# Linear attention feeding a gated layer: unread matrix products after each group of products in the first batch's attention

## The chip, the cores and the metric

The kernel runs on one core of one Trainium2 chip. The metric is the device time of one execution in microseconds (us). Before the change it is 1277.1 us, the median of 3 runs (1275.62 to 1277.16).

The core's engines named here are TensorE (PE in the profile; PEld is its weight load), VectorE (DVE), ScalarE (ACT), GpSimd (POOL) and SyncE (SP), which here only issues DMA transfers. Each engine works through its own instruction list in order. TensorE's clock is granted at one of two levels, 1.2 GHz (0.50 in the profile) or 2.4 GHz (1.00).

## The reference

Attention is linear: queries and keys go through random features, so that a head needs one 128x64 matrix `kv` and no table of scores. Its output, 4608 tokens by 512, is the input of a gated layer.

```
def phi(x):                                    # x is q or k, scaled by 1/64**0.25
    proj = einsum('bhsd,md->bhsm', x, omega)   # 8 x 8 x 576 x 128
    h = proj - sum(x * x, -1) / 2
    h = h - max(h, -1)
    return exp(h) / sqrt(m)
q_p, k_p = phi(q_s), phi(k_s)
kv  = einsum('bhsm,bhsd->bhmd', k_p, v)
z   = sum(k_p, axis=2)
num = einsum('bhsm,bhmd->bhsd', q_p, kv)
den = einsum('bhsm,bhm->bhs', q_p, z) + 1e-6
x   = (num / den).transpose(0, 2, 1, 3).reshape(4608, 512)
out = (sigmoid(x @ w_gate) * (x @ w_val)) @ w_out     # w_gate, w_val: 512 x 1536; w_out: 1536 x 512
```

All arrays are float32; the weights arrive as float64 bits and are converted on the chip.

## The kernel before

**Heads and tokens.** Eight heads are four pairs `p`; a pair's two heads share the 128 partitions. Batches go two at a time (`u`), as nine tiles of 128 tokens, the fifth shared by both batches. A task is one pair and one batch, of keys (`keys`) or queries (`queries`); `norms` is the task that squares and sums the rows of q or k for all pairs.

**Products of a task.** `projected` splits its operand into a high part `hi` (ACT) and a rest `lo` (POOL), and multiplies groups of one or two tiles with the split feature matrix, three products of 256 columns to a tile (lines 522 to 524, bank `pp`). DVE takes the maxima `mx` (L527) and combines them with the norms (`hm`, then `nb` for keys or `sub` and `h` for queries). For keys, ACT's exponential writes `kp`, and ten fp32 products of 66 columns make `pkv` (L570). For queries, TensorE transposes `h` into `pt` (L601), ACT's exponential writes `qp`, fp32 products of 66 columns with `kv` make `pn` (L613), DVE divides into `x` (L624), TensorE transposes that into `px` (L630), and ACT copies it and sends it to DRAM (`xT`).

**Gated layer.** `first_pass` reads `xT` back (`xr`, L214), splits it into `xe` (ACT, POOL) and makes four column tiles of the gate and value products (`gv`, L236), in the gaps of the attention; `second_pass` and `last` do the rest after it. The weights are converted from float64 bits by DVE and POOL (tiles `e` and `c`, L78 to L96), and split into `wh`, `wl`.

**Order.** The tasks are generators, up to six at a time. Until the first 256 tokens of all pairs are through (`ready(Q)`), only the first batch's eight tasks run, with one step of the weights' conversion after every 16 steps; this is the loop at lines 697 to 701, called the first stage here. After it, 14 attention steps go with every half of a column tile. The order in which instructions then stand on each engine is made by the tile framework's scheduler, which may move them past each other as far as their data allow.

**PSUM.** Eight banks: six have the tag `at`, two the tag `gv`. `any_bank` gives attention the next bank of `cycle`, or an `at` bank where `cycle` is empty. In the first stage `cycle` is `at, at, at, gv` (L695), so that attention uses all eight.

Of the kernel before, what the change touches and what calls it, by code (L numbers as in the profile page):

```python
# [20 lines left out]
P = 128  # L21
# [23 lines left out]
ACTIVE = {"n": 1, "k": 3, "q": 4}  # L45
AT_ONCE = 6
AHEAD = 8
EVERY = 16
FROM = 14
N_TAIL = 3  # L50
# [49 lines left out]
def attn_glu_kernel(ctx: ExitStack, tc, qT, kT, qn, kn, va, om, ident, w, out):  # L100
# [23 lines left out]
    def bank(tag, name):  # L124
        return ps.tile([P, 512], F32, tag=tag, bufs=banks[tag], name=name)
# [346 lines left out]
    def span(name, b):  # L472

        g = GROUPS[name][b]
        return g[0][0], g[-1][-1] + 1

    def norms(pool, name, u, b, src):

        t0, t1 = span(name, b)
        s = pool.tile([P, MID + 1, H], F32, tag="ss", bufs=2, name=f"ss{name}{u}_{b}")[:, : t1 - t0]  # L480
        for t in range(t0, t1):
            x = pool.tile([P, DM], F32, tag="nat", bufs=3, name=f"nat{name}{u}_{t}")
            nc.sync.dma_start(out=x, in_=src[u, :, t, :])
            x2 = pool.tile([P, DM], F32, tag="x2", bufs=2, name=f"x2{name}{u}_{t}")
            nc.scalar.activation(out=x2, in_=x, func=AF.Square)
            yield
            nc.vector.tensor_reduce(
                out=s[:, t - t0, :], in_=x2.rearrange("p (h d) -> p h d", d=D), axis=AX.X, op=ALU.add
            )
        sq = pool.tile([P, MID + 1, H], F32, tag="sq", bufs=6, name=f"sq{name}{u}_{b}")  # L490
        nc.vector.tensor_scalar(
            out=sq[:, : t1 - t0], in0=s, scalar1=SCALE * SCALE / 2.0, scalar2=None, op0=ALU.mult
        )
        sqs[name, u, b] = sq
        yield

    def projected(pool, name, u, p, b, src):


        t0, t1 = span(name, b)  # L500
        n = (t1 - t0) * P
        raw = pool.tile([P, (MID + 1) * P], F32, tag="raw", bufs=RAWS, name=f"raw{name}{u}_{p}_{b}")
        nc.sync.dma_start(out=raw[:, :n], in_=src[u, p, :, t0 * P : t1 * P])
        yield None
        while (name, u, b) not in sqs:
            yield None
        sq = sqs[name, u, b]
        for tiles in GROUPS[name][b]:
            id_ = f"{name}{u}_{p}_{tiles[0]}"
            nt = len(tiles)  # L510
            hi, lo = (
                pool.tile([P, 2 * P], F32R, tag=tag, bufs=SPLITS, name=f"{tag}{id_}")[:, : nt * P]
                for tag in ("hi", "lo")
            )
            o = (tiles[0] - t0) * P
            split(nc, hi, lo, raw[:, o : o + nt * P], lo_engine=nc.gpsimd)
            yield None
            pp = any_bank(f"pp{id_}")[:, : nt * 2 * M]
            for i, t in enumerate(tiles):
                c = slice(i * P, (i + 1) * P)  # L520
                o = pp[:, i * 2 * M : (i + 1) * 2 * M]
                nc.tensor.matmul(o, lhsT=lo[:, c], rhs=omH, start=True, stop=False)  # L522
                nc.tensor.matmul(o, lhsT=hi[:, c], rhs=omL, start=False, stop=False)  # L523
                nc.tensor.matmul(o, lhsT=hi[:, c], rhs=omH, start=False, stop=True)  # L524
            pp = pp.rearrange("p (i m) -> p i m", m=M)
            mx = pool.tile([P, 2 * nt], F32, tag="mx", bufs=6, name=f"mx{id_}")
            nc.vector.tensor_reduce(out=mx, in_=pp, axis=AX.X, op=ALU.max)  # L527
            s = sq[:, tiles[0] - t0 : tiles[-1] + 1 - t0, 2 * p : 2 * p + 2]
            hm = pool.tile([P, nt, 2], F32, tag="hm", bufs=6, name=f"hm{id_}")
            nc.vector.scalar_tensor_tensor(  # L530
                out=hm, in0=mx.rearrange("p (t h) -> p t h", h=2), scalar=SCALE, in1=s,
                op0=ALU.mult, op1=ALU.subtract,
            )
            yield id_, tiles, pp, hm, s

    def keys(pool, u, p, b):
        v = None
        kp = {}
        if b:
            kp[MID] = kmid.pop((u, p))  # L540
        for g in projected(pool, "k", u, p, b, kT):
            if g is None:
                yield
                continue
            id_, tiles, pp, hm, s = g
            nt = len(tiles)
            if v is None:
                v = pool.tile([P, MID + 1, 2, E], F32, tag="v", bufs=VS, name=f"v{u}_{p}_{b}")
                nc.sync.dma_start(out=v, in_=va[u, p, b])
            nb = pool.tile([P, nt, 2], F32, tag="nb", bufs=6, name=f"nb{id_}")  # L550
            nc.vector.scalar_tensor_tensor(  # L551
                out=nb, in0=s, scalar=-1.0, in1=hm, op0=ALU.mult, op1=ALU.subtract
            )
            if tiles[0] == MID:
                x = pool.tile([P, 2 * nt, M], F32, tag="kmid", bufs=4, name=f"kmid{id_}")
                kmid[u, p] = x
            else:
                x = pool.tile([P, 2 * nt, M], F32, tag="kp", bufs=KPS, name=f"kp{id_}")
            for i, t in enumerate(tiles):
                kp[t] = x[:, 2 * i : 2 * i + 2, :]  # L560
                for h in range(2):
                    nc.scalar.activation(  # L562
                        out=kp[t][:, h, :], in_=pp[:, 2 * i + h, :], func=AF.Exp,
                        bias=nb[:, i, h : h + 1], scale=SCALE,
                    )
            yield
        pkv = any_bank(f"pkv{u}_{p}_{b}")[:, : 2 * E].rearrange("p (h e) -> p h e", h=2)
        for h in range(2):
            for i in range(MID + 1):
                nc.tensor.matmul(  # L570
                    pkv[:, h, :], lhsT=kp[b * MID + i][:, h, :], rhs=v[:, i, h, :],
                    start=(i == 0), stop=(i == MID),
                )
        kv = pool.tile([P, 2, E], F32, tag="kv", bufs=15, name=f"kv{u}_{p}_{b}")
        nc.scalar.activation(out=kv, in_=pkv, func=AF.Copy)
        kvs[u, p, b] = kv
        yield

    def queries(pool, u, p, b):
        for g in projected(pool, "q", u, p, b, qT):  # L580
# [25 lines left out]
            for i, t in enumerate(tiles):  # L606
# [4 lines left out]
                for h in range(2):  # L611
                    for bb, r in mine:
                        nc.tensor.matmul(  # L613
                            pn[r, 2 * i + h, :], lhsT=qp[:, 2 * i + h, r], rhs=kvs[u, p, bb][:, h, :],
                            start=True, stop=True,
                        )
            den = pool.tile([P, n, 1], F32, tag="den", bufs=6, name=f"den{id_}")
            nc.vector.tensor_scalar(
                out=den, in0=pn[:, :, D : D + 1], scalar1=EPS, scalar2=None, op0=ALU.add
# [66 lines left out]
    with tc.tile_pool(name="early", bufs=1) as early:  # L686
        gates = first_pass()
        with tc.tile_pool(name="a", bufs=1, side="right") as pool:
# [3 lines left out]
                return pool.tile([P, 7 * WP], U32, tag="cv", bufs=2, name=name)  # L692

            conv = first_weights(early, tiles)
            cycle[:] = ["at", "at", "at", "gv"]  # L695
            n = 0
            while not ready(Q):
                next(steps, None)
                n += 1
                if n % EVERY == 0:  # L700
                    next(conv, None)
            cycle.clear()
            later = convert_weights(tiles, range(N_LATE - N_TAIL))
            n = credit = 0
            while not ready(B * S):
# [147 lines left out]
```

## Time and profile before

| | |
|---|---|
| median of 3 runs | 1277.1 us |
| the profiled execution | 1272.84 us, its span 1271.0 us, mean clock 0.955 |
| TensorE busy | 1180.4 us, 93% of the span |
| DVE, ACT, POOL busy | 900.3, 600.5, 505.9 us |
| TensorE's share of the chain that ended last | 71% |

The busy share of TensorE is high over the whole, but not in the first 94 us. From 200 us on its clock is at 1.00 nearly throughout (a dip lies around 500 to 540 us). A record of TensorE shows the time from its own start to its modelled end, and records overlap: how long one holds the engine is read from the chain, where each piece is counted only to the start of the next. An fp32 product has two records, one of the split (fp32r) form has one: the 256 products of L570 with `kp` are 512 records.

### The profile page before, as it was taken

The page shows a single profiled execution, that of the slowest core. Times are in us where ns is not written, and L with a number is a line of the kernel's source. Part 1 is how long each engine was busy: PE and PEld are TensorE (multiplying, and loading weights), DVE is VectorE, ACT ScalarE, POOL GpSimd, SP SyncE. Part 2 cuts the span into 40 slices and gives each one's busy share as a digit, 9 for nine tenths or more (in the row PEclk, how much of TensorE's full clock was granted, in tenths as well). Part 3 has the DMA queues.
Part 4 walks back from the last instruction along what each step waited for, and adds up shares of the span by engine and source line. Part 5 has one row for each costly group of instructions (what it writes and reads, how often), then busy time and mean ns, then how long its engine had stood idle before and what let it go on. Part 6 is the DMA issues. An engine that isn't in the chain of part 4 may idle for free.

```text
span 1271.0 us, 24153 instructions
## 1 busy us (share of the span) xinstructions
PE 1180.4 (93%) x8828; PEld 1115.5 (88%) x8828; DVE 900.3 (71%) x2054; ACT 600.5 (47%) x1220; POOL 505.9 (40%) x548
## 2 busy tenths in 40 slices
PE   4879889989999998788999999999999899999998
PEld 4868888878888897666899999999998799999998
DVE  6778888899897665386566565665667777777674
ACT  5448777877776665232422222322224344343331
POOL 3533444344342322133176666666666421111110
PEclk8768889999999999599999999999999999999999
DMA  7655577776854440176423333233328676666553
GB/s 255 214 171 187 164 241 267 226 238 221 293 204 148 123 129 34 55 252 229 152 88 122 132 137 111 100 121 121 135 85 282 199 221 189 211 193 185 183 183 108
DMA packets 104950, 219.43 MB, mean 173 GB/s; under 512 B 11136, under 2 KB 42112, under 8 KB 103040
## 3 DMA queue, kind: packets, MB, share of 16 engines
q1 hardware_dynamic: 87984, 198.94, 47.3%
q10 hardware_dynamic: 16848, 18.95, 4.3%
q8 instruction: 70, 1.15, 0.4%
q14 instruction: 48, 0.39, 0.1%
HBM read 141.82 MB, written 76.02 MB: 171 GB/s over the span
## 4 chain that ended last, share of the span: by engine, by line
PE 71%; DVE 12%; POOL 5%; DMA 5%; issue 4%; ACT 3%; SPq 1%; ACTq 0%; DVEq 0%; POOLq 0%
PE gw L336 25%; PE po L449 20%; PE gv L236 9%; PE pnq L613 4%; PE pkv L570 4%; PE ptq L601 2%; DMA u<-w 1%; POOL xe L71 1%; DVE mxk L527 1%; DVE mxq L527 1%; DVE hq L590 1%; PE ppq L522 1%; DMA natk<-kn 1%; PE ppq L524 1%; PE ppq L523 1%
## 5 line engine op out<-in xcount | busy, mean ns | idle before, releaser
L336 PE MATMUL gw<-xl,u 128*128 128x256 f32 x3024 | 362.8, 282 | 7.0 <-DVE u L316 6.8
L336 PEld LDWEIGHTS gw<-xl,u 128*128 128x128 f32 x3024 | 361.2, 190 | 8.6 <-DVE u L316 8.0
L449 PE MATMUL po<-u,yh 128*128 128x256 f32 x1512 | 272.1, 283 | 0.0
L449 PEld LDWEIGHTS po<-u,yh 128*128 128x128 f32 x1512 | 234.7, 191 | 0.0
L449 PE MATMUL po<-u,yl 128*128 128x256 f32 x756 | 214.3, 283 | 5.6 <-POOL yl L71 4.1
L236 PE MATMUL gv<-xe,wh 128*128 128x512 f32 (+1 forms) x640 | 201.0, 389 | 4.2 <-POOL xe L71 3.9
L70 ACT ACTIVATE yh<-yr 128x896 fp32r<-128x896 f32 x108 | 99.8, 949 | 161.7 <-PE po L449 74.7
L449 PEld LDWEIGHTS po<-u,yl 128*128 128x128 f32 x756 | 144.3, 191 | 6.2 <-POOL yl L71 4.3
L236 PEld LDWEIGHTS gv<-xe,wh 128*128 128x128 f32 x640 | 118.0, 195 | 24.2 <-POOL xe L71 7.7
L236 PE MATMUL gv<-xe,wl 128*128 128x512 f32 (+1 forms) x320 | 125.3, 394 | 14.0 <-DVE ye L261 8.5
L71 POOL TENSOR_TENSOR yl<-yr,yh 128x896 fp32r<-128x896 f32 x18 | 39.6, 2199 | 214.7 <-PE po L449 114.6
L71 DVE TENSOR_TENSOR yl<-yr,yh 128x896 fp32r<-128x896 f32 x90 | 97.4, 1102 | 23.6 <-ACT yh L70 12.2
L316 DVE TENSOR_TENSOR u<-gw,p 128x256 f32<-128x256 f32 x144 | 60.6, 421 | 58.2 <-PE gw L336 50.2
L440 DVE TENSOR_TENSOR yr<-yr 128x128 f32<-128x128 f32 x144 | 66.1, 493 | 48.7 <-DMA yr<-ye 48.3
L71 POOL TENSOR_TENSOR loq<-rawq,hiq 128x256 fp32r<-128x256 f32 (+1 forms) x80 | 57.9, 736 | 98.7 <-ACT hiq L70 90.5
L71 POOL TENSOR_TENSOR lok<-rawk,hik 128x256 fp32r<-128x256 f32 (+1 forms) x80 | 55.4, 702 | 103.7 <-ACT hik L70 103.5
L613 PEld LDWEIGHTS pnq<-kv,qpq 128*128 128x128 f32 (+1 forms) x640 | 75.9, 200 | 11.3 <-ACT qpq L603 8.3
L236 PEld LDWEIGHTS gv<-xe,wl 128*128 128x128 f32 x320 | 62.6, 197 | 25.9 <-DVE ye L261 10.8
L613 PE MATMUL pnq<-kv,qpq 128*128 128x66 f32 (+1 forms) x640 | 79.7, 284 | 4.5 <-ACT qpq L603 4.4
L570 PE MATMUL pkv<-v,kpk 128*128 128x66 f32 x512 | 77.9, 288 | 3.0 <-ACT kpk L562 2.9
L570 PEld LDWEIGHTS pkv<-v,kpk 128*128 128x128 f32 x512 | 72.1, 206 | 6.5 <-ACT kpk L562 5.0
L562 ACT ACTIVATE kpk<-ppk,nbk 128x128 f32<-128x128 f32 x256 | 71.2, 384 | 11.9 <-DVE nbk L551 10.0
(113 smaller groups left out, 2229.9 us busy)
## 6 DMA issues: line engine op xcount, KB each, us to landing
yl<-yl SPq DMA_DIRECT2D x36, 896.0 KB, 3.7
yr<-yl SPq DMA_DIRECT2D x72, 448.0 KB, 3.8
xr<-xT SPq DMA_DIRECT2D x68, 256.0 KB, 4.4
c<-w SPq DMA_DIRECT2D x22, 512.0 KB, 5.7
w<-c SPq DMA_DIRECT2D x11, 1024.0 KB, 4.1
v<-va SPq DMA_DIRECT2D x32, 330.0 KB, 3.4
natk<-kn SPq DMA_DIRECT2D x36, 256.0 KB, 3.6
natq<-qn SPq DMA_DIRECT2D x36, 256.0 KB, 4.0
```

Of the source, the lines that this page charges most:

```text
L70: nc.scalar.activation(out=hi, in_=x, func=AF.Copy)
L71: (lo_engine or nc.vector).tensor_tensor(out=lo, in0=x, in1=hi.bitcast(F32), op=ALU.subtract)
L236: nc.tensor.matmul(gv, lhsT=u[:, s], rhs=v, start=(m == 0), stop=(m == 3 * KC - 1))
L316: return nc.vector.tensor_tensor(out=o, in0=a, in1=b, op=ALU.add)
L336: nc.tensor.matmul(o, lhsT=u[:, k, s], rhs=v[:, kc, :], start=(first and m == 0), stop=(m == 5), skip_group_check=not first,)
L440: nc.vector.tensor_tensor(out=raw[:, o], in0=raw[:, a], in1=raw[:, b], op=op)
L449: nc.tensor.matmul(o, lhsT=u[:, i, :], rhs=v[:, k, :], start=(j + m == 0 and n in (1, 6, 5, 4)), stop=(j == NPAIR - 1 and m == 2), skip_gr ...
L527: nc.vector.tensor_reduce(out=mx, in_=pp, axis=AX.X, op=ALU.max)
L562: nc.scalar.activation(out=kp[t][:, h, :], in_=pp[:, 2 * i + h, :], func=AF.Exp, bias=nb[:, i, h : h + 1], scale=SCALE,)
L570: nc.tensor.matmul(pkv[:, h, :], lhsT=kp[b * MID + i][:, h, :], rhs=v[:, i, h, :], start=(i == 0), stop=(i == MID),)
L601: nc.tensor.transpose(out=pt[:, i, :], in_=h_sb[:, i, :], identity=id_sb)
L613: nc.tensor.matmul(pn[r, 2 * i + h, :], lhsT=qp[:, 2 * i + h, r], rhs=kvs[u, p, bb][:, h, :], start=True, stop=True,)
```

## The change

A bank of the tag `gv` is held during the first stage under the name `unread`, and `keep_busy` issues four products into it after each group of products: after `pp` (256 columns, the split form), after `pkv` and after `pn` (128 columns, fp32, against the identity). Nothing reads the bank. In exchange attention has the six `at` banks alone in the first stage.

```
+UNREAD = 4
...
+    unread = []
+
+    def keep_busy(a, b, n):
+
+        for o in unread:
+            for _ in range(n):
+                nc.tensor.matmul(o[:, : b.shape[1]], lhsT=a, rhs=b, start=True, stop=True)
...
                 nc.tensor.matmul(o, lhsT=hi[:, c], rhs=omH, start=False, stop=True)
+            keep_busy(hi[:, :P], omH, UNREAD)
...
+        keep_busy(kp[b * MID][:, 0, :], id_sb, UNREAD)
         kv = pool.tile([P, 2, E], F32, tag="kv", bufs=15, name=f"kv{u}_{p}_{b}")
...
+            keep_busy(qp[:, 0, :], id_sb, UNREAD)
             den = pool.tile([P, n, 1], F32, tag="den", bufs=6, name=f"den{id_}")
...
             conv = first_weights(early, tiles)
-            cycle[:] = ["at", "at", "at", "gv"]
+            unread.append(bank("gv", "unread"))
...
-            cycle.clear()
+            unread.clear()
```

The scheduler puts the added products where their operands let it, and orders the rest anew. 120 products are added: 76 of 256 columns (19 groups `pp`) and 44 of 128 columns (4 `pkv`, 7 `pn`). Three places follow; in the names the first number is the pair, the second the first tile of the group.

TensorE, before, where the keys' last groups meet `pkv`:

```order
L522 MATMUL ppk_0_4_337<-omH,lok_0_4_303 128x256
L523 MATMUL ppk_0_4_337<-omL,hik_0_4_302 128x256
L524 MATMUL ppk_0_4_337<-omH,hik_0_4_302 128x256
L570 MATMUL pkv_1_0_353<-v_1_0_155,kpk_1_0_159 128x66 x2
L570 MATMUL pkv_2_0_366<-v_2_0_175,kpk_2_0_179 128x66 x2
```

TensorE, now, at the same place:

```order
L484 MATMUL unread<-omH,hik_0_4_327 128x256 x4
L484 MATMUL unread<-id_sb,kpk_1_0_164 128x128 x4
L531 MATMUL ppk_1_4_336<-omH,lok_1_4_320 128x256
L532 MATMUL ppk_1_4_336<-omL,hik_1_4_319 128x256
L533 MATMUL ppk_1_4_336<-omH,hik_1_4_319 128x256
L484 MATMUL unread<-id_sb,kpk_2_0_188 128x128 x3
```

With six banks the groups of the fifth tile stand behind the first exponentials, and the unread products of `pkv` come ahead of `pkv` itself.

TensorE, before, at the second group of queries (pairs 1, 2, 0):

```order
L601 MATMUL ptq_1_2_699<-id_sb,hq_1_2_653 128x128 x4
L601 MATMUL ptq_2_2_706<-id_sb,hq_2_2_668 128x128 x4
L601 MATMUL ptq_0_2_713<-id_sb,hq_0_2_683 128x128 x4
L613 MATMUL pnq_1_2_722<-kv_1_0_364,qpq_1_2_704 128x66 x4
L613 MATMUL pnq_2_2_733<-kv_2_0_377,qpq_2_2_711 128x66 x4
```

TensorE, now, at the same place:

```order
L612 MATMUL ptq_1_2_800<-id_sb,hq_1_2_746 128x128 x4
L484 MATMUL unread<-id_sb,qpq_1_2_805 128x128 x4
L237 MATMUL gv_0_0_954<-xe_0_942,wl_113 128x256
L237 MATMUL gv_0_0_954<-xe_0_942,wh_112 128x256
L612 MATMUL ptq_2_2_807<-id_sb,hq_2_2_765 128x128 x4
L237 MATMUL gv_0_0_954<-xe_0_942,wh_112 128x256
L237 MATMUL gv_0_0_954<-xe_1_945,wl_113 128x256
```

The first gate product, which needs `xe_0`, now stands ahead of two of the three transposes; before it stood behind the transpose `px` of pair 3.

DVE, before, between the maxima and `h` of pair 3's first queries (rows of `e` are the weights' conversion, `ss` the norms):

```order
L527 TENSOR_REDUCE mxq_3_0_784<-ppq_3_0_777 128x4
L94 SCALAR_TENSOR_TENSOR e_685<-e_685 128x512
L530 SCALAR_TENSOR_TENSOR hmq_3_0_786<-mxq_3_0_784,sqq_0_351 128x4
L487 TENSOR_REDUCE ssk_1_854<-x2k_8_934 128x8
L588 TENSOR_TENSOR subq_3_0_788<-sqq_0_351,hmq_3_0_786 128x4
L78 TENSOR_SCALAR e_997<-e_997 128x512
L590 SCALAR_TENSOR_TENSOR hq_3_0_790<-ppq_3_0_777,subq_3_0_788 128x512
```

DVE, now, at the same place:

```order
L537 TENSOR_REDUCE mxq_3_0_901<-ppq_3_0_890 128x4
L93 TENSOR_SCALAR e_1118<-e_1118 128x512
L540 SCALAR_TENSOR_TENSOR hmq_3_0_903<-mxq_3_0_901,sqq_0_388 128x4
L500 TENSOR_SCALAR sqq_1_1333<-ssq_1_1167 128x40
L95 SCALAR_TENSOR_TENSOR e_1118<-e_1118 128x512
L599 TENSOR_TENSOR subq_3_0_905<-sqq_0_388,hmq_3_0_903 128x4
L496 TENSOR_REDUCE ssk_0_1422<-x2k_0_1425 128x8
L601 SCALAR_TENSOR_TENSOR hq_3_0_907<-ppq_3_0_890,subq_3_0_905 128x512
```

The same place of the attention stands further down DVE's list: ahead of `hq_3_0` there are now 48 pieces of conversion and 19 pieces of norms, where there were 37 and 13. `e_1118` is the fourth column tile's weights, `e_997` of before, which was only begun here. From the middle of the first pass on, the lists are the same on every engine.

## Rows read from the trace of the kernel before

**Rows 1.** Windows by stage: us, busy PE, PEld, DVE, ACT, POOL, clock, DMA, GB/s.
```profile
23.00:41.00 18.00, 15.71 (x69) 14.85 (x68) 13.45 (x35) 10.89 (x37) 6.22 (x6) 0.50 0.57 191
41.00:51.00 10.00, 6.85 (x46) 5.83 (x44) 9.31 (x24) 5.23 (x15) 7.36 (x10) 0.90 0.53 163
51.00:64.00 13.00, 11.50 (x67) 10.71 (x67) 10.21 (x28) 6.85 (x20) 6.95 (x7) 0.72 0.84 266
64.00:78.00 14.00, 9.59 (x44) 8.95 (x44) 9.64 (x25) 5.87 (x14) 4.43 (x6) 0.62 0.41 128
78.00:94.00 16.00, 11.90 (x63) 10.54 (x64) 12.82 (x30) 7.29 (x15) 5.27 (x6) 0.71 0.66 209
94.00:200.00 106.00, 93.22 (x713) 89.47 (x714) 88.94 (x252) 79.50 (x190) 45.96 (x52) 0.89 0.61 200
200.00:500.00 300.00, 291.79 (x2084) 257.12 (x2083) 243.96 (x681) 219.06 (x510) 107.77 (x130) 1.00 0.58 191
```

**Rows 2.** Windows around a dense stretch of TensorE, same columns.
```profile
32.00:39.00 7.00, 7.00 (x33) 7.00 (x34) 4.52 (x10) 2.54 (x9) 2.76 (x3) 0.50 0.76 260
39.00:43.00 4.00, 3.90 (x18) 3.60 (x18) 1.71 (x3) 1.75 (x6) 2.93 (x4) 0.50 0.03 10
43.00:45.00 2.00, 2.00 (x19) 1.99 (x17) 2.00 (x6) 1.54 (x6) 2.00 (x5) 0.99 0.00 0
```

**Rows 3.** Chain that ended last, 0 to 94 us: start us, us, what, count.
```profile
31.93 7.95 PE pkv L570 x36
54.53 1.18 PE pkv L570 x6
56.34 0.22 PE ppk L523
64.37 1.97 PE ptq L601 x8
66.34 5.03 PE pnq L613 x24
78.14 1.10 PE ptq L601 x4
79.92 1.98 PE pnq L613 x8
85.08 2.63 PE gv L236 x13
```

**Rows 4.** The same chain later, where the clock is 1.00.
```profile
87.71 0.45 PE ptq L601 x4
94.68 0.12 PE ppk L522
100.29 0.62 PE pkv L570 x6
```

**Rows 5.** Timeline of DVE: start us, us, line, operation, shapes.
```profile
64.84 0.41 DVE L78 TENSOR_SCALAR e<-e 128x512 uint32<-128x512 uint32 x1
65.17 0.68 DVE L487 TENSOR_REDUCE ssk<-x2k 128x8 f32<-128x512 f32 x1
71.89 0.66 DVE L88 SCALAR_TENSOR_TENSOR e<-e 128x512 uint32<-128x512 uint32 x1
```

**Rows 6.** Timeline of POOL: start us, us, line, operation [idle before, releaser].
```profile
67.88 2.29 POOL L71 TENSOR_TENSOR xe<-xr,xe 128x256 fp32r<-128x256 f32 x3 [4.85 <-ACT xe L70]
```

**Rows 7.** Chain, 104 to 113 us.
```profile
104.88 1.27 POOL c L96
106.16 3.36 issue
109.55 1.26 POOL wl L71
112.77 0.58 PE ppk L522
```

## Prediction

> **What bounds the kernel now.** I read the windows by stage first. Up to 94 us TensorE is neither full nor fast: from 23 to 94 us it is busy 55.6 of 71 us, and its granted clock is 0.50 from 23 to 41 us and 0.62 to 0.90 in the stages after [rows 1]. From 200 to 500 us it is busy 291.8 of 300 us at 1.00, and bounds the kernel there [rows 1]. So time that the first stage saves or loses should arrive at the end, unless the stretch of 94 to 200 us, where TensorE still idles 12.8 us [rows 1], takes it up.
>
> Then the chain of waits: in the first stage most of its long pieces are TensorE's, and nearly all of them at 0.50, such as 36 records of `pkv` in 7.95 us and 24 of `pn` in 5.03 us [rows 3]. Between them lie DVE's maxima, `h` and divisions. What the change can gain is the difference between these pieces and the same work at 1.00; what it can lose is the time of the added products where they stand on this chain, and what the new order does to DVE and to the transfers.
>
> What raised the clock is seen where TensorE is dense. From 32 to 39 us TensorE is busy 7.00 of 7 us with fp32 products of 66 columns, and the clock stays 0.50. From 39 to 43 us it is as full, mostly with split products of 256 columns, and from 43 to 45 us the clock is 0.99 [rows 2]. So the split products count, and long runs of 66-column products don't. The 76 unread products of 256 columns are of the kind that raised it; for the 44 of 128 columns, fp32, the trace has no row.
>
> **The change part by part.** *Prices.* A split product costs 0.12 us at 1.00 and 0.21 at 0.50 [rows 4, 3]; a record of 66 columns 0.62/6 = 0.10 and 7.95/36 = 0.22 [rows 4, 3]; a transpose of 128 columns 0.45/4 = 0.11 and 1.97/8 = 0.25 [rows 4, 3]. An unread fp32 product is two records of 128 columns. The nearest row by width is the transpose, so I take 0.11 and 0.25 a record. The bounds are the 66-column record, 0.10 and 0.22, and twice it, 0.20 and 0.43, if time goes with columns. All unread work is then 76 x 0.12 + 88 x 0.11 = 18.8 us at 1.00, or 76 x 0.21 + 88 x 0.25 = 38 us at 0.50; TensorE's idle time from 23 to 94 us is 15.4 us [rows 1], so it can't all be hidden.
>
> *Term A, the clock on the chain.* At 1.00 the 36 records of `pkv` would take 3.7 us instead of 7.95: 4.2 saved. In the piece from 53 to 60 us there are 19 split products (0.09 saved each) and 8 records of `pkv` (0.10 each): 2.5. The eight transposes and 24 `pn` records at 64 to 71 us: 1.1 + 2.5 = 3.6. In the rest, 12 split products, four transposes, eight `pn` records and the 13 gate products at 85 us: 1.1 + 0.6 + 1.1 + 1.1 = 3.9 [rows 3, 4]. Together 14.2. I take the first two whole, since dense unread products now stand right ahead of both, and half of the other two, since TensorE must wait there (below): 10.4 saved. The bounds are 0 and 14.2.
>
> The Trainium skill (TensorE: Matmul & The Clock Gate, Part 4) says that transposes don't count as busy for the clock as other products do. By that rule the transposes that stand between the unread products help nothing, and if the later half of A goes with them, 3.7 us less is saved and the sum is -1.0, 1276.1; the trace agrees in so far as the eight transposes at 64 us ran at 0.25 us each [rows 3].
>
> *Term B, unread products on the chain.* Not all of them lie there. Those behind the first groups up to 22 us run while TensorE waits for the exponentials, and those ahead of `pkv` stand before a wait for the fifth tile's exponentials, which ended only at 31.9 us [rows 3]; I cost them at nothing. On the chain remain: four behind `ppk_3_0`, then between `pn_0_0` and the end of `ppq_0_2` 12 split products and 16 records, then 16 records behind two `pn` and four split products ahead of `ppq_3_0`: 20 x 0.12 + 32 x 0.11 = 5.9, say 6.0 added at 1.00; 20 x 0.21 + 32 x 0.25 = 12.2 at 0.50; 18.0 with the wide bound.
>
> *Term C, the new order.* On DVE 11 more pieces of conversion and 6 more of norms stand ahead of `hq_3_0`. Two of six pieces of a conversion take 0.66 us, four 0.41, so 0.49 on average [rows 5]; 11 x 0.49 + 6 x 0.68 = 9.5 us. DVE's idle time from 23 to 78 us is 12.4 us [rows 1], so between nothing and all of it is hidden; I take half, 4.7 added. On TensorE the gate product now waits for `xe_0` with two transposes, their `pn` and all of pair 3 queued behind it. In the trace of before the transposes began at 64.37 us [rows 3] and the first `xe` was done some 0.75 us after 67.88 [rows 6], 4.3 us later; that is one end, nothing the other. Since `xe_0` stands earlier on ACT's list too, I take 2.0. The bank trade lets the fifth tile's three groups wait for the first exponentials; DVE wants their maxima only after 24 us, so nothing, or at most those three groups at 0.50 (9 x 0.21 = 1.9).
>
> *Term D, what is given back.* The 9.5 us of DVE's work done early is not due again between 94 and 200 us. There the chain ran from 104.88 to 112.77 us through POOL's conversion, 3.36 us of issue and the fourth tile's `wl`, with TensorE waiting at its end [rows 7], and the clock was low after it. These conversions are now over before the first stage ends. Nothing to 9.5 us comes back; I take 7.0, since that chain alone is 7.9 us.
>
> *Sum.* -10.4 + 6.0 + 4.7 + 2.0 - 7.0 = -4.7 us. The durations are of the profiled execution, 1272.84 us, which would become 1268.1; it lies 4.3 below the median of the runs, and I forecast against the median: 1277.1 - 4.7 = 1272.4.
>
> **The rivals.** *Same.* Only half of D comes back, because attention's next batch starts later and POOL and DVE find other waits: -4.7 + 3.5 = -1.2, 1275.9. For it: four of the five terms are of the size of the result, and DVE is 84% busy from 94 to 200 us [rows 1]. Against: the long POOL chain does go.
>
> *Slower: pair 3 comes late.* DVE's early work isn't hidden (9.5 instead of 4.7) and nothing comes back, since TensorE, which bounds the kernel from 200 us on, has lost the time by then: -10.4 + 6.0 + 9.5 + 2.0 = +7.1, 1284.2. It decides from the point where `h` of pair 3 comes more than about 7 us later than at 77 us. For it: the conversions stand between a maximum and its `h`, on the chain itself. Against: DVE's 12.4 us of idle time.
>
> *The unread products don't keep the clock up.* A is 0, B goes at 0.50: 12.2 + 6.7 - 7.0 = +11.9, 1289.0. For it: seven full microseconds at 0.50 [rows 2]. Against: the split products, which did raise it.
>
> *Everything is at 1.00.* A is 14.2, DVE's work is hidden: -14.2 + 6.0 + 2.0 - 7.0 = -13.2, 1263.9. For it: with the gaps filled there would be no stretch without products. Against: TensorE still waits for DVE and `xe`. Beside it, the Trainium skill (same page, Part 1, What's actually happening) says that the clock follows how busy the array has been, whatever it does; by that rule this would be the result, and it has the chance given here. The trace differs: the full stretch at 0.50 speaks for a finer measure than busy time.
>
> **How the numbers follow.** The forecast has 0.33, everything at 1.00 0.10, same 0.25, pair 3 late 0.25, clock not kept 0.07. A difference of 0.2%, 2.6 us, is about what a measurement of this kernel can tell from no change. Faster by more than that is 0.33 + 0.10 = 0.43; within it 0.25; slower 0.32. The range reaches from the fast rival to just past the late one, 1264 to 1286: it leaves out the unkept clock and part of the outer cases, about 2 in 10. The forecast's own range is 1269 to 1275.
>
> **What would show it.** Right for A: `pkv` at about 0.10 us a record from 32 us on, and a clock above 0.8 from 41 to 64 us. For B: unread fp32 records 0.11 us apart. For C: TensorE idle ahead of the first gate product, and `hq_3_0` between 77 and 82 us. For D: no wait of TensorE for POOL around 110 us. Wrong if `pkv` stays at 0.22 us a record, or if the 200 us mark is reached with fewer TensorE records done than before, the unread ones left out (289 + 713 = 1002 from 23 us on) [rows 1].

## The result and the profile after

The changed kernel takes 1279.9 us (median of 20 runs, 1273.9 to 1288.2), the kernel before, run beside it, 1275.7 (20 runs). The ratio is 1.0042, 95% interval [1.0023, 1.0061]: slower by about 5.4 us where 4.7 us of gain were forecast. The range, 1264 to 1286, holds the time. The profiled execution took 1279.19 us, its span 1277.1, at a mean granted clock of 0.969 (before 0.955).

These are the windows of the changed kernel by stage, with the columns of [rows 1], the first 23 us ahead of them; the same stretch of the kernel before, which [rows 1] doesn't have, stands alone behind.

```profile
0.00:23.00 23.00, 12.07 (x81) 11.87 (x81) 12.76 (x28) 10.23 (x24) 8.39 (x15) 1.00 0.83 281
23.00:41.00 18.00, 15.59 (x116) 14.91 (x115) 16.65 (x36) 12.33 (x40) 9.15 (x10) 0.91 0.56 195
41.00:51.00 10.00, 5.98 (x38) 5.44 (x37) 10.00 (x23) 5.13 (x12) 5.99 (x7) 0.83 0.72 221
51.00:64.00 13.00, 13.00 (x114) 12.81 (x114) 12.23 (x33) 7.35 (x19) 5.71 (x6) 1.00 0.86 284
64.00:78.00 14.00, 11.20 (x91) 10.20 (x89) 13.31 (x31) 7.58 (x16) 8.64 (x9) 1.00 0.56 178
78.00:94.00 16.00, 8.47 (x37) 7.60 (x37) 11.91 (x31) 7.02 (x15) 3.95 (x4) 0.68 0.74 233
94.00:200.00 106.00, 92.65 (x720) 88.01 (x720) 89.63 (x244) 76.04 (x188) 45.70 (x52) 0.92 0.63 202
200.00:500.00 300.00, 286.18 (x2025) 251.68 (x2025) 233.72 (x660) 209.66 (x495) 105.14 (x127) 0.99 0.57 182
```

```profile
0.00:23.00 23.00, 7.22 (x44) 7.05 (x45) 12.88 (x28) 10.30 (x25) 8.60 (x15) 0.92 0.85 284
```

The clock did what was forecast: 0.83 or more in every stage from 23 to 78 us, where before it was 0.50 to 0.90. After 78 us it is low again, 0.68, as before (0.71) [rows 1]. Now read TensorE's busy time. In the first 23 us it grew by 4.85 us: the unread products there stand in time that TensorE waited anyway. From 23 to 94 us it is 54.2 us, before 55.6: the useful records got faster, and unread ones took the time that this freed. Of the 164 unread records 44 lie ahead of 23 us. Without the other 120, TensorE has done 1116 - 120 = 996 records from 23 to 200 us, before 1002 [rows 1], and from 200 to 500 us 2025 instead of 2084. That is the sign that the prediction named for being wrong, though at 200 us it hangs on 6 records of 1002.

Read DVE's column as well. From 23 to 78 us DVE is busy 16.65 + 10.00 + 12.23 + 13.31 = 52.2 of 55 us, before 42.6 [rows 1]: the idle time in which its early work was to hide is nearly used up. The chain that ended last shows the same. Of its pieces up to 94 us TensorE had 37.7 us before and has 15.9 now, 6.8 of them unread products; DVE's conversions had 6.1 and have 16.5. In this execution TensorE is no longer what most of the first stage waits for.

Next TensorE's timeline around pair 3 in the changed kernel (start, us, line, operation, tiles; in brackets idle time ahead and what ended it).

```profile
32.12 0.44 PE L580 MATMUL pkv<-v,kmidk 128*128 128x66 f32 x2 [0.19 <-ACT kmidk L572]
...
36.37 0.39 PE L531 MATMUL ppk<-omH,lok 128*128 128x256 f32 x1
...
67.78 0.39 PE L237 MATMUL gv<-xe,wl 128*128 128x256 f32 x1 [0.48 <-ACT xe L71]
...
70.81 1.90 PE L624 MATMUL pnq<-kv,qpq 128*128 128x66 f32 x16
72.54 1.11 PE L484 MATMUL unread<-id_sb,qpq 128*128 128x128 f32 x8
...
80.74 0.70 PE L612 MATMUL ptq<-id_sb,hq 128*128 128x128 f32 x4 [3.24 <-DVE hq L601]
...
85.47 2.02 PE L484 MATMUL unread<-id_sb,qpq 128*128 128x128 f32 x8
...
94.47 0.84 PE L612 MATMUL ptq<-id_sb,hq 128*128 128x128 f32 x4 [2.94 <-DVE hq L601]
```

The 36 records of `pkv` last from 32.12 to 36.37 us, 0.12 each, and 16 of `pn` from 70.81 to 72.54, 0.11 each: half of what [rows 3] show. But look where the unread ones stand and where TensorE waits: they come behind `pn`, where the next work is ready, and at 85.47 us they take 2 us at the low clock. The waits, 3.24 and 2.94 us, stand ahead of transposes, for DVE's `h`. What DVE does meanwhile is its own timeline, from the maximum of pair 3 to its `h`:

```profile
77.54 0.69 DVE L537 TENSOR_REDUCE mxq<-ppq 128x4 f32<-128x512 f32 x1
78.14 0.42 DVE L93 TENSOR_SCALAR e<-e 128x512 uint32<-128x512 uint32 x1
...
78.64 0.68 DVE L95 SCALAR_TENSOR_TENSOR e<-e 128x512 f32<-128x512 uint32 x1
...
79.31 0.68 DVE L496 TENSOR_REDUCE ssk<-x2k 128x8 f32<-128x512 f32 x1
79.91 0.68 DVE L601 SCALAR_TENSOR_TENSOR hq<-ppq,subq 128x512 f32<-128x512 f32 x1
```

Two pieces of conversion and one of a norm (`ss`) stand between them, as many as before; new is what stands further ahead.

`pkv` ends at 36.37 us, 3.5 us earlier than before (39.88 [rows 3]). This lead is gone at the first queries. TensorE there, in the kernel before:

```profile
46.50 0.66 PE L601 MATMUL ptq<-id_sb,hq 128*128 128x128 f32 x4 [1.31 <-DVE hq L590]
48.14 1.25 PE L601 MATMUL ptq<-id_sb,hq 128*128 128x128 f32 x8 [0.98 <-DVE hq L590]
...
53.03 0.40 PE L630 MATMUL pxq<-id_sb,xq 128*128 128x128 f32 x2
```

and in the changed kernel, with DVE's `h` of the second and third group behind it:

```profile
45.32 0.63 PE L612 MATMUL ptq<-id_sb,hq 128*128 128x128 f32 x4 [2.37 <-DVE hmq L540]
47.60 1.22 PE L484 MATMUL unread<-id_sb,qpq 128*128 128x128 f32 x4 [1.65 <-ACT qpq L614]
48.62 1.06 PE L612 MATMUL ptq<-id_sb,hq 128*128 128x128 f32 x4
49.47 2.07 PE L484 MATMUL unread<-id_sb,qpq 128*128 128x128 f32 x12
51.38 0.60 PE L612 MATMUL ptq<-id_sb,hq 128*128 128x128 f32 x4
...
56.33 0.38 PE L642 MATMUL pxq<-id_sb,xq 128*128 128x128 f32 x2
```

```profile
46.68 0.68 DVE L601 SCALAR_TENSOR_TENSOR hq<-ppq,subq 128x512 f32<-128x512 f32 x1
...
47.35 1.77 DVE L89 SCALAR_TENSOR_TENSOR e<-e 128x512 uint32<-128x512 uint32 x1
...
49.70 0.68 DVE L601 SCALAR_TENSOR_TENSOR hq<-ppq,subq 128x512 f32<-128x512 f32 x1
```

The first transposes wait for DVE and start only 1.2 us earlier than before. The second and third `h` are done at 47.36 and 50.38 us, but their transposes start at 48.62 and 51.38: 16 unread records stand ahead of them, 2.9 us of TensorE's time, and the first of these waits for ACT's exponential, which they read. The third `h` is late itself, behind a conversion. So the first `x` is transposed at 56.33 us, 3.3 us later than before. Whether the loss is the new order's or the products' own is the first question.

### The profile page after: what moved, and what is told of

Its sections match the earlier page's. It is cut to its first block, busy times and chain, and to the rows that moved or that the text cites. A ratio compares the mean times of both kernels' runs of the same rounds, so it can differ in the third digit from the quotient of the medians.

```text
span 1277.1 us, 24484 instructions
## 1 busy us (share of the span) xinstructions
PE 1188.9 (93%) x8992; PEld 1122.8 (88%) x8992; DVE 909.3 (71%) x2054; ACT 598.4 (47%) x1218; POOL 508.5 (40%) x548
## 4 chain that ended last, share of the span: by engine, by line
PE 64%; DVE 12%; DMA 7%; issue 6%; POOL 6%; ACT 3%; SPq 1%; ACTq 0%; DVEq 0%; POOLq 0%
PE gw L337 25%; PE po L450 20%; PE gv L237 7%; PE pnq L624 3%; PE pkv L580 3%; DMA xr<-xT 2%; PE ptq L612 2%; DMA xT<-xsq 2%; DVE mxq L537 1%; DVE mxk L537 1%; DMA natk<-kn 1%; POOL xe L72 1%; DVE hq L601 1%; DMA u<-w 1%; POOL c L97 1%
## 5 line engine op out<-in xcount | busy, mean ns | idle before, releaser
L237 PE MATMUL gv<-xe,wh 128*128 128x512 f32 (+1 forms) x640 | 204.5, 395 | 5.3 <-POOL xe L72 4.5
L441 DVE TENSOR_TENSOR yr<-yr 128x128 f32<-128x128 f32 x144 | 70.4, 524 | 53.8 <-DMA yr<-ye 53.4
L72 DVE TENSOR_TENSOR yl<-yr,yh 128x896 fp32r<-128x896 f32 x90 | 96.6, 1101 | 14.7 <-ACT yh L71 14.5
L624 PEld LDWEIGHTS pnq<-kv,qpq 128*128 128x128 f32 (+1 forms) x640 | 72.8, 194 | 15.1 <-ACT qpq L614 10.2
L624 PE MATMUL pnq<-kv,qpq 128*128 128x66 f32 (+1 forms) x640 | 76.6, 277 | 7.9 <-ACT qpq L614 6.6
L572 ACT ACTIVATE kpk<-ppk,nbk 128x128 f32<-128x128 f32 x256 | 71.3, 387 | 17.8 <-DVE nbk L561 16.3
L580 PE MATMUL pkv<-v,kpk 128*128 128x66 f32 x512 | 71.2, 271 | 3.2 <-ACT kpk L572 3.2
L367 ACT ACTIVATE gl<-gl 128x768 f32<-128x768 f32 x36 | 30.5, 846 | 91.9 <-DVE gl L317 91.9
```

Source lines behind the costliest of these rows:

```text
L72: (lo_engine or nc.vector).tensor_tensor(out=lo, in0=x, in1=hi.bitcast(F32), op=ALU.subtract)
L237: nc.tensor.matmul(gv, lhsT=u[:, s], rhs=v, start=(m == 0), stop=(m == 3 * KC - 1))
L367: pin(nc.scalar.activation(out=g[:, 1:], in_=g[:, 1:], func=AF.Sigmoid))
L441: nc.vector.tensor_tensor(out=raw[:, o], in0=raw[:, a], in1=raw[:, b], op=op)
L572: nc.scalar.activation(out=kp[t][:, h, :], in_=pp[:, 2 * i + h, :], func=AF.Exp, bias=nb[:, i, h : h + 1], scale=SCALE,)
L580: nc.tensor.matmul(pkv[:, h, :], lhsT=kp[b * MID + i][:, h, :], rhs=v[:, i, h, :], start=(i == 0), stop=(i == MID),)
```

## The experiments

Two measures are used beside the time. *Clock lost* is a run's time x (1 - its mean granted clock), as a mean over the runs; *rest* is time less clock lost. Below, both are given against the runs of the kernel before made beside each kernel (clock lost 55.0 to 56.2 us, rest 1216.5 to 1219.3); for the change, whose neighbours have no clock on record, against the mean of all these, 55.5 and 1218.4. It is a way to split the time, and no proof by itself: where TensorE waits, a higher clock makes clock lost smaller and rest larger by as much, and the time stays. So a larger rest is not yet a cost; the ratio decides. An interval given below for a difference of two kernels is worked out from their two intervals.

| kernel | unread | clock lost, us | rest, us | ratio, 95% interval |
|---|---|---|---|---|
| the change | 120 | -15.5 | +21.4 | 1.0042 [1.0023, 1.0061] |
| e1 its order alone | 0 | +3.8 | -0.2 | 1.0022 [1.0000, 1.0044] |
| e2 products, order of before | 120 | -11.2 | +13.5 | 1.0008 [0.9981, 1.0035] |
| e3 banks alone | 0 | -5.3 | +1.9 | 0.9969 [0.9943, 0.9995] |
| e4 DVE held back | 120 | -14.1 | +22.4 | 1.0064 [1.0036, 1.0091] |
| e5 first nine, order of before | 36 | -0.6 | +0.2 | 0.9994 [0.9967, 1.0021] |
| e6 split only, order of before | 76 | -1.4 | +2.1 | 1.0002 [0.9973, 1.0031] |
| e7 first nine, banks | 36 | -9.3 | +4.4 | 0.9953 [0.9932, 0.9975] |
| e8 products, order of e3 | 120 | -13.0 | +19.3 | 1.0056 [1.0033, 1.0078] |
| e9 eight each, order of before | 240 | -17.5 | +35.5 | 1.0144 [1.0110, 1.0177] |
| e10 narrow, order of before | 120 | -1.7 | +16.3 | 1.0116 [1.0071, 1.0162] |
| e11 fp32 only, order of before | 44 | -11.9 | +15.8 | 1.0030 [1.0001, 1.0059] |
| e12 nine, the change's order | 36 | +0.7 | +8.0 | 1.0066 [1.0039, 1.0094] |
| e13 in waits, order of e3 | 86 | -13.4 | +9.0 | 0.9961 [0.9936, 0.9986] |
| e14 in waits and nine | 122 | -19.1 | +11.4 | 0.9941 [0.9909, 0.9973] |
| e15 nine behind, order of e3 | 36 | -9.9 | +4.2 | 0.9958 [0.9926, 0.9990] |

**Order and products apart (e1 to e3).** An order is held by edges between the instructions of an engine, without a wait:

```diff
+        for a, b in zip(line, line[1:]):
+            tc.add_manual_dep(
+                b, a.name, mybir.DependencyInfo(mybir.DependencyClass.NoSync, ...
```

e1 has `UNREAD = 0` and the change's order:

> The order of the changed kernel on all five engines, held by a table, without one unread product. Theory 'order': the conversions and norms that now stand ahead of pair 3 and of the next keys on DVE and ACT cost some 10 us of the first stage, the unread products gave part of it back through the clock; without them the kernel is slower than before by more than the change was: +8 to +12 us (ratio 1.006 to 1.010), with a clock of about 0.5 from 23 to 41 us as before. Rival 'products': the loss is the time of the products themselves, the order is harmless: -2 to +2 us (0.998 to 1.002). Rival 'banks': six banks in rotation instead of eight cost the time: +4 to +6 us.

e2 has the order of before and, since its eight banks are all in use, each group's own bank:

```diff
+            keep_busy(pp[:, : 2 * M], hi[:, :P], omH, UNREAD, ahead=True)
             for i, t in enumerate(tiles):
...
+        keep_busy(both[:, P * 2 : P * 3], kp[b * MID][:, 0, :], id_sb, UNREAD)
...
+            keep_busy(both[:, P * 3 :], qp[:, 0, :], id_sb, UNREAD)
```

> The order of the kernel before on all five engines, held by a table, and its eight banks; the 120 unread products are added, four at each of the same groups: those of the keys' and queries' projections go ahead of their group into its own bank, the others behind it into columns of its bank that nothing uses. Theory 'order': the gain of the clock is had without the loss: -3 to -8 us (ratio 0.994 to 0.998), first-stage clock above 0.8 from 32 us. Rival 'products': their time on TensorE's path outweighs the clock, as in the change: +3 to +7 us. Rival 'banks': as 'order' here, -3 to -8 us, since no bank is taken.

e3 is the change with `UNREAD = 0`, the order left to the scheduler:

> The change with no unread product at all (0 instead of 4): what is left is the trade of banks (six in rotation instead of eight, and one held back) and the order that comes of it, which has 4 more pieces of conversion and 3 more of norms ahead of the h of pair 3 than before (the change: 11 and 8 more). Theory 'order': a share of its loss by the share of the work moved ahead, +2 to +5 us (ratio 1.0015 to 1.004). Rival 'products': -1 to +1 us. Rival 'banks': all of the loss and more, +4 to +8 us.

Each theory failed somewhere. The order alone costs 2.8 us (0 to 5.6), less than "order" said, and against e3 6.8 (2.5 to 11.1); the products alone gain nothing; and the banks with the order that comes of them are a gain of 4 us (0.6 to 7.3). The chain of e2 shows where the clock's gain goes:

```profile
33.35 1.81 PE pkv L484 x8
35.16 1.46 PE pkv L582 x12
36.63 0.94 PE pkv L484 x8
37.57 1.29 PE pkv L582 x12
38.86 0.94 PE pkv L484 x8
```

From 35.16 us on `pkv` runs at 1.00, but three lots of unread products (line 484) stand between its groups, 3.7 us, and the whole ends at 39.80 us; before it ended at 31.93 + 7.95 = 39.88 [rows 3].

e2 has a wait, too, that the change hasn't. Its unread products behind `pn` write into the bank of `pn`, and DVE's `den`, which reads that bank, waits for them (40 to 100 us; us, times, longest):

```profile
DVE denq L633 <- PE pnq L484: 11.3, 7, 3.0
```

In the kernel before `den` waited 7.9 us, for `pn` itself, at the low clock. In the change the unread bank is one of its own; `den` waits 1.3 us there, for `pn` itself. What follows on e8 to e11, which are placed like e2, holds for this placing.

The windows of e1 show what its order costs:

```profile
51.00:64.00 13.00, 12.38 (x62) 11.71 (x60) 8.54 (x26) 6.70 (x17) 4.09 (x4) 0.53 0.73 248
...
78.00:94.00 16.00, 10.66 (x46) 9.16 (x46) 13.76 (x36) 6.54 (x13) 3.26 (x3) 0.61 0.68 208
94.00:112.00 18.00, 13.01 (x61) 11.92 (x60) 15.03 (x33) 10.49 (x20) 4.44 (x5) 0.52 0.79 244
```

The clock is still 0.52 at 94 to 112 us. By the table the order's whole cost goes with the clock: 3.8 us more of it lost than before, 9.1 more than in e3, and no more rest.

**Is it DVE's early work, and which products pay (e4 to e7).** e4 is the change with edges that keep each conversion or norm on DVE behind the attention piece that it followed before:

```diff
+        hold_back(tc)
```

> The change with all its 120 unread products and its six banks, but on DVE each piece of conversion or norm of the first part may not stand ahead of the attention piece that it stood behind in the kernel before: 37 pieces of conversion and 15 of norms ahead of the h of pair 3 (before 37 and 15, the change 48 and 23). Theory 'order': DVE's early pieces are what the change lost by; -1 to +1 us against the kernel before (ratio 0.999 to 1.001), h of pair 3 at 78 us or earlier. Rival 'TensorE's time': the unread products take 19.4 us of TensorE's time and save 10.7 us of slowness and 1.4 us of idle time up to the second pass in the trace of the change, and DVE isn't the bound: +4 to +7 us, as the change.

It is slower than the kernel before by 0.64%, as the change or worse, though `h` of pair 3 is done at 78.98 us, 1.6 earlier than in the change. With the products there, giving DVE its old order repairs nothing. That DVE's early work costs nothing doesn't follow: in e4's trace the chain up to 94 us goes back to TensorE, with 9.2 us of unread products on it, where the change had 6.8, and 8.8 of conversions instead of 16.5. e5 and e6 are e2 with fewer products:

```diff
-        for _ in unread:
+        if ahead and len(ADDED) < FIRST * n:
```

> The order and banks of the kernel before, held by a table, with four unread products ahead of the first nine groups alone (36 products of 256 columns; the other 84 are left out). Theory 'TensorE's time': an unread product pays where TensorE would have waited anyway; 36 x 0.118 = 4.2 us go into the 15.8 us that TensorE idles in the first 23 us, and the clock of the 18 us that follow rises from 0.50 to 0.66 or more, which took 3 us of slowness away in e2_products_alone: -3 to -6 us (ratio 0.995 to 0.998). Rival 'lost later': what the first stage gains, a wait on DVE or a transfer behind it takes back: -1 to +1 us.

```diff
-        for _ in unread:
+        if ahead:
```

> As e2_products_alone (the order and banks of the kernel before), with the 76 split products ahead of their groups and without the 44 fp32 products behind pkv and pn. Theory 'TensorE's time': the fp32 products are 88 records at 0.118 = 10.4 us, nearly all between products that are waited for; without them the chain is shorter by about as much, and if the split products hold the clock by themselves (slowness not over 45 us up to the second pass, 42.4 with both, 57.6 before) the kernel is faster: -4 to -8 us (ratio 0.994 to 0.997). Rival 'fp32 products hold the clock': the clock from 64 to 94 us is 0.7 or less as before, and the time is within 2 us of before. Rival 'lost later': -1 to +1 us.

e5 costs nothing and wins nothing. In e6 the split products win 1.4 us of clock, no more than the noise, and the time stays: the theory missed, and in these places the split products do not do what the prediction read from [rows 2]. e7 is the change with products at nine groups:

```diff
-            for _ in range(n):
+            for _ in range(n if len(added) < FIRST * n else 0):
```

> The change as it is (its banks, the scheduler free), but unread products at the first nine groups alone, 36 instead of 120; the order on the other engines is then that of e3_banks_alone but for a few rows. Theory 'TensorE's time': the 4.0 us that e3_banks_alone is faster, and 3 to 6 us more for the clock from 23 to 41 us: -7 to -10 us (ratio 0.992 to 0.9945). Rival 'lost later': as e3_banks_alone, -3 to -5 us (0.996 to 0.998).

At 0.9953 it is faster than both kernels, though less than forecast, and not surely more so than e3.

**What a product costs (e8 to e11).** e8 is e2's placing with e3's banks and order; e9 has `UNREAD = 8`; e10 cuts every product to 64 columns; e11 keeps the fp32 ones alone:

```diff
+                x = nc.tensor.matmul(o[:, :64], lhsT=a, rhs=b[:, :64], start=True, stop=True)
...
-        for _ in unread:
+        if not ahead:
```

> The banks and the order of e3_banks_alone, held by a table on all five engines, with all 120 unread products, placed as in e2_products_alone. Measure beside the time: clock lost, which is a run's time x (1 - its mean granted clock), as a mean over the runs; it is 55.5 us in the kernel before, 40.0 in the change, 59.1 in e1, 44.2 in e2 and 50.0 in e3. Theory 'price': time moves by the clock lost plus the unread products' own 19.4 us, of which at most 5.6 falls into waits; the clock lost comes down from 50 to 40 to 44, so against e3 +4 to +13, and against the kernel before 0 to +9 us (ratio 1.000 to 1.007). Rival 'order': the loss is the move from the order of e3 to that of the change (e1 minus e3, 6.8 us), and the products are harmless or better: as e3 or faster, -3 to -8 us (0.994 to 0.998).

> As e2_products_alone (the order and banks of the kernel before), with eight unread products at each place instead of four: 240, 38.8 us at full clock. Theory 'price': the clock can give back little more than the four did (clock lost 44.2 us, of which some 15 lie between 500 us and the second pass and are out of reach), and the waits are filled: +12 to +22 us (ratio 1.009 to 1.017). Rival 'hidden': the products stand where TensorE waits anyway and the first four cost nothing either: -2 to +5 us.

> As e2_products_alone, with unread products of 64 columns instead of 256 (split) and 128 (fp32). Theory 'price': if time goes with columns the 120 take 7 us or less instead of 19.4; if the clock stays up as in e2 (clock lost about 44) the kernel is faster than before by 4 to 8 us (ratio 0.994 to 0.997); if the clock goes with the columns too, clock lost is 50 to 56 and the time within 3 us of before. Rival 'hidden': their time has no say; as e2, 0 to +3 us.

> As e2_products_alone, with the 44 fp32 products behind pkv and pn alone (10.4 us at full clock); the 76 split ones, which by themselves left the clock lost at 54.3 us (e6_split_only), are left out. Reading of rows 2 in the prediction: only split products raise the clock; then clock lost stays at 53 to 56 and the time goes up by most of 10.4 us: +6 to +10 (ratio 1.005 to 1.008). Theory 'price, fp32 products hold the clock': clock lost 43 to 48, and the time within 3 us of before (0.998 to 1.002).

e8 and e9 came as "price" said: with order and banks fixed, 120 products turn e3's 0.9969 into 1.0056 (11.1 us, 6.7 to 15.5), and 240 make the kernel of before 18 us slower. e11 contradicts the reading that only split products raise the clock: 44 fp32 products of 128 columns win 11.9 us of clock, as much as the 120 of e2, and the kernel is no faster for the 76 that are left out. Its time, +3.8 us, lies between the two forecasts. e10 missed both its arms, since a narrow record is hardly shorter. In its chain eight records of unread products of 64 columns take

```profile
39.32 1.70 PE pkv L484 x8
...
61.74 0.89 PE pnq L484 x8
```

0.21 us each at the low clock and 0.11 at 1.00, against 0.94/8 = 0.12 for 128 columns in e2. Its rest grows as in e2, it wins no clock, and it is 1.2% slower. Its TensorE and that of e2 from 23 to 94 us, e10 first:

```profile
23.00:94.00 71.00, 61.84 (x372) 58.67 (x373) 47.57 (x115) 31.59 (x87) 26.13 (x29) 0.71 0.50 162
```

```profile
23.00:94.00 71.00, 57.51 (x397) 53.94 (x396) 51.68 (x127) 33.36 (x87) 29.44 (x31) 0.84 0.54 173
```

The busier of the two has the lower clock. The Trainium skill (TensorE: Matmul & The Clock Gate, Part 1, What's actually happening) has the clock follow how busy the engine has been recently. These two rows do not decide on that: the busy time here is that of records, which last longer at the lower clock (0.21 us instead of 0.11 above) and about as long for 64 columns as for 128. The same caution holds for the prediction's use of [rows 2].

**Place or order (e12 to e15).** e12 holds the change's order and keeps the first 36 products, four behind each of nine groups; e15 does the same in e3's order:

```diff
+                if len(ADDED) < FIRST * n:
```

> The change's own order on all five engines and its banks, held by a table, with the unread products of the first nine groups alone (36, each four right behind its group); the 84 later ones are left out. Clock lost (a run's time x (1 - its mean granted clock)) is 59.1 us in e1 (this order without products) and 40.0 in the change; the rest of the time is 1219.1 and 1239.8. Theory 'price': the 36 stand in waits and leave the rest of the time at 1217 to 1223, as in e5 and e7; what clock they win (0 to 9 us) comes off: -6 to +3 us against the kernel before (ratio 0.995 to 1.002), and the 84 later ones are what brings the change to +5.4, by 2 to 11 us. Rival 'order': the products have no say in this order; as the change or e1, +3 to +6 us.

> The order and banks of e3_banks_alone, held by a table, with the 36 products of the first nine groups each four right behind its group, as e12_change_order_nine had them; e7_first_nine_banks, nearly the same order, had two fours ahead of the first group and three others together. Theory 'place': behind a group they stand ahead of the next group, whose maximum DVE waits for; the rest of the time rises by 4 to 7 us over e3's 1221.3 as in e12 (1226.3 against 1219.1), and the kernel is 3 to 7 us slower than e7: -3 to +1 us against the kernel before (ratio 0.998 to 1.001). Rival 'order': e12's loss came from the change's order, and here the 36 are harmless: -4 to -8 us (0.994 to 0.997).

e13 and e14 put products of two constants ahead of six groups for which TensorE waits:

```diff
+UNREAD = {"ptq0_1_0": 12, "pxq0_1_0": 8, "ptq0_1_2": 6, "ptq0_3_0": 28, "pxq0_3_0": 8, "ptq0_3_2": 24}
...
+            keep_busy(pt[:, : 2 * M], UNREAD.get(f"pt{id_}", 0))
+            keep_busy(px[:, 2 * M :], UNREAD.get(f"px{id_}", 0))
```

> The order and banks of e3_banks_alone, held by a table, with 86 unread products of 256 columns that need no other engine (both operands are constants), ahead of six groups for which TensorE waits for DVE in the trace of e3: 12 ahead of the first transposes of the queries (waited 2.2 us), 8 and 8 ahead of the x of pairs 1 and 3 (0.7 and 1.7), 6 ahead of ptq_1_2 (0.8), 28 ahead of ptq_3_0 (3.4) and 24 ahead of ptq_3_2 (3.6). They take 10.3 us at full clock, the waits are 12.4. Theory 'place': in a wait a product costs nothing; the rest of the time (time less clock lost) stays within 4 us of e3's 1221.3 and the clock lost falls from 50.0 to 42 to 47: -5 to -12 us against the kernel before (ratio 0.991 to 0.996). Rival 'any product costs its time': the rest rises by 9 us or more, and the kernel is at 0 to +5 us (1.000 to 1.004).

> As e13_in_waits, with four more products ahead of each of the first nine groups, as e5_first_nine had them: 122 in all, 14.6 us, about as many as the change has. Theory 'place': -6 to -13 us (ratio 0.990 to 0.995), clock lost 38 to 45. Rival 'any product costs its time': +2 to +9 us (1.002 to 1.007).

e8 and e14 share order and banks, and their intervals lie far apart: 1.0056 and 0.9941. But place is not all that differs. e8 has 76 split products ahead of their groups and 44 fp32 ones behind theirs, 164 records, and `den` waits for these as in e2 (10.4 us); the 122 of e14 are split ones of constants, ahead of waits or of the first nine groups, 122 records. How much of the 14.7 us between them is place, how much the kind and number of products and how much the wait of `den`, no run separates. Waits of TensorE from 64 to 94 us (us, times, longest), e8 first, then e14:

```profile
PE ptq L614 <- DVE hq L603: 4.6, 2, 4.1
PE pxq L645 <- DVE xq L639: 1.6, 1, 1.6
...
PE pnq L627 <- ACT qpq L616: 0.7, 1, 0.7
```

```profile
PE ptq L613 <- DVE hq L600: 2.8, 4, 1.1
PE pnq L625 <- ACT qpq L615: 2.4, 2, 1.8
PE pxq L644 <- DVE xq L636: 0.7, 1, 0.7
```

The waits for DVE are partly filled, the one for ACT has grown. From 64 to 112 us the clock of e14 holds at 0.91 and more:

```profile
64.00:78.00 14.00, 11.68 (x95) 11.03 (x96) 12.39 (x32) 5.89 (x13) 6.23 (x6) 1.00 0.49 156
78.00:94.00 16.00, 11.45 (x75) 10.09 (x75) 13.85 (x34) 9.72 (x17) 6.81 (x6) 0.91 0.77 241
94.00:112.00 18.00, 17.44 (x146) 17.16 (x146) 15.26 (x42) 13.84 (x43) 7.35 (x10) 0.98 0.68 211
```

The size of "place" missed: the rest rises over e3 by 7.1 us in e13 and 9.5 in e14, for products of 10.3 and 14.6, where little was forecast. And against e3, which has their order and no product at all, none of them is shown to be faster: e13 is at 0.9961, e15 at 0.9958, e14 at 0.9941, e3 at 0.9969. The 3.6 us between e3 and e14 have an interval of 5.3 us to either side. What is shown is that the products of e8 cost more time than they win; of these no net cost is seen.

Order is shown by e12 and e15, alike but for it: 1.0066 and 0.9958, 13.8 us apart (8.4 to 19.2), 10.6 us of it clock. "Place" was wrong for the first nine groups, where behind costs no more than ahead (e15, e7). But e12 is also 5.6 us slower (1.1 to 10.1) than e1, the same order without products, and slower than both its forecasts: in the change's order even the first 36 are not free.

## Why the prediction was wrong

*Step that failed: the sum of terms A and B.* It has the products save 10.4 us of TensorE's time on the path and add 6.0, together -4.4. Measured with the order held, they save nothing in any order: +2.5 us in the change's (the change against e1, -1.2 to 6.2), +11.1 in e3's (e8), +1.0 in that of before (e2, -2.4 to 4.5). C and D, put at -0.3, came to +2.8 (e1, 0 to 5.6). So of the 10.1 us between forecast and result some 6.9 lie in A and B, 3.1 in C and D.

*Term A* had the clock right and the path wrong. The clock rose: 15.5 us less of it lost than before, 19.1 less than in e1, and `pkv` ran at 0.12 us a record, forecast 0.10. But the time saved on TensorE was taken to arrive whole, and it does not: `pkv` ended 3.5 us earlier and the transposes after it began 1.2 us earlier, because they wait for DVE, which is busy 52.2 of 55 us; up to 94 us the chain of the changed kernel has no `pkv` on it. The reason given for the clock does not hold as it stands: in the places of e2 the fp32 products carry it (e11) and hardly the split ones (e6), while split ones in waits win 8.1 us over e3 (e13).

*Term B* cost every product at nothing that was not on its list, and the list misses the 16 records ahead of the first queries' transposes, 2.9 us, with the wait for the exponential that comes with them. That the unread products on the chain up to 94 us take 6.8 us, close to 6.0, is luck: these 16 are 3 of the 6.8. How the 6.9 us divide between A and B is not shown; rest and clock lost can't tell, as said above.

*Term C* was right in its places. TensorE waits for `xe` ahead of the first gate product, though 0.48 us and not 2.0, and `h` of pair 3 was done at 79.91 + 0.68 = 80.59 us, inside 77 to 82. Half of the added 9.5 us of DVE's work was to be hidden; nearly all of it went into DVE's idle time, and DVE became the one that is waited for. Taking the early work back did not help (e4), and the order by itself costs clock (e1 against e3). Bank trade and the order that comes with it, put at 0, are a gain of 4 us (e3).

*Term D*, -7.0, is not seen. From 94 to 200 us TensorE did 720 records, before 713. The wait for POOL around 110 us [rows 7] is gone, as said; what TensorE waits for from 94 to 130 us is now (us, times, longest)

```profile
PE ptq L612 <- DVE hq L601: 3.6, 2, 2.9
PE gv L237 <- ACT ge L256: 0.8, 1, 0.8
```

so pair 3's second `h` took its place. All the signs that the prediction named for being right came, those of `pkv` (0.12), the clock, the gate product, `h` of pair 3 and POOL. They show that each thing happened at its place, not that its time arrives at the end.

*The rivals.* The late pair 3 gave 1284.2 and the right sign. Its first transposes start at 80.74 instead of 78.14 us [rows 3], 2.6 later and not 7, but its second at 94.47 instead of 87.71 [rows 4], 6.8 later. So part of it was there; its mechanism, DVE's early work, is not shown to be the cause, since e4 is no faster. "Clock not kept" fell at once, and "everything at 1.00" with 0.68 from 78 to 94 us; "same" rested on half of D.

*Open:* how the loss divides between A and B; why the order and banks of e3 lose 5.3 us less clock than before; by which engine the change's order lets the clock fall; whether that order with products in waits would do as e14 does, and what fp32 products in waits or split ones behind `pn` would do, which wasn't tried.

## What to carry to other kernels

A faster engine saves time only as far as the path stays with it: before adding up what a higher clock saves, ask which engine is waited for next, and how much idle time that one has left. For every product added only to keep TensorE's clock up, count three things: its own time, the operand it waits for, and who waits for its bank. Products of constants ahead of an instruction that waits anyway (e13, e14) showed no net cost here; that they gain over the same order without them is not shown. Ask, too, what a scheduler will do with added instructions: the order that it made here (e1) lost 9.1 us more clock than that of the same banks without products (e3). And compare a change with the same order held, or order and work can't be told apart.

## What the runs showed that I had not expected

A record of an fp32 product costs about the same at 64 columns (0.11 us) as at 128 (0.12) with the clock at 1.00, so cutting columns to 64 saved next to nothing (e10). With the same places and counts, the 128- and 256-column products lost 44.2 us to the clock and the 64-column ones 54.5.
